# Splitting the last weight load of a decode kernel into eight transfers of fewer partitions

## The chip, the core and the metric

The kernel runs on one core of a Trainium2 chip. The metric is device time in microseconds (us) of one execution; the time given is the median of several runs. The core has TensorE (PE; its weight loads are PEld), VectorE (DVE), ScalarE (ACT), GpSimd (POOL) and SyncE (SP), each with its own instruction stream, and 16 DMA engines that carry the transfers which SyncE and ScalarE issue.

## The reference

One token is decoded. Two branches read the same normalised vector and are added:

```
xn  = layernorm(x)                                  # x: 1 x 1024
q   = xn @ wq                                       # 32 heads of 128
A   = softmax(q k^T / sqrt(128)) v, then @ wo       # 4 KV heads, 65536 cached positions
h   = gelu(layernorm(xn) @ w1)                      # 1024 -> 1024
x1  = xn + shift(h) @ w2                            # four quarters shifted by 1 or 2 places
B   = x1 + gelu(layernorm(x1) @ w3) @ w4            # 1024 -> 3584 -> 1024
out = x + A + B
```

The inputs are bf16. The two caches have 64 MiB each, wq and wo 8 MiB each, w3 and w4 7 MiB each, w1 and w2 2 MiB each. All are read once.

## The kernel before

The host-side code writes out five instruction streams (queues) by hand. A helper records for every buffer object who wrote and who read it, and puts a wait on a semaphore ahead of an instruction only where it is needed and not yet known to be fulfilled. Each load has its own semaphore (a "channel"), and a load is complete when its semaphore has had 16 increments.

The keys and values stream through two slots of 4 MiB each in the tile KV, by 32 loads issued by SyncE. A loop over 32 steps (`NT`) transposes keys on VectorE into the tile WX, multiplies them with the query on TensorE, takes a running maximum and an exponential, and accumulates the values. The weights share these tiles: when the slots come free at the end of the loop, w1 and w2 go into WX, w3 into the first half of KV, wo into the second half, and last w4 into WX again, over w1, w2 and the transposed keys.

A weight of R rows is laid out with R/128 successive rows on each of 128 partitions (`load_rows`, line 328, is one transfer over all 128 partitions). For w4, 3584 x 1024, a partition holds 28 rows of 2 KB. It is loaded in three parts (line 638 on):

```
w4_parts = [(0, 20), (20, 6), (26, 2)]
```

that is 40, 12 and 4 KB a partition, 5120, 1536 and 512 KB in all, each with a buffer object and a semaphore of its own. Their issues wait for the last readers and writers of what they overwrite; behind them SyncE has only the output's store (line 672).

The end of the kernel runs so. After the loop TensorE multiplies with w1 and w2, VectorE does the activation and the second layer norm, TensorE multiplies with w3, and the result `gh_bf` is ready some 24 us before w4 is there. `out_rows` (line 454) then multiplies one row of weights at a time with four matmuls, which add into the PSUM tile `OUT_ps`: first the 32 rows of wo, then, by `w4_pe(i)`, the rows of part 0, 1 and 2 of w4, 80, 24 and 8 matmuls. Each `w4_pe(i)` waits for the semaphore of its part. VectorE casts the sum into `orow` (line 671), SyncE stores it, and the kernel ends.

Of the kernel before, what the change touches and what calls it, by code (L numbers as in the profile page):

```python
# [118 lines left out]
def _deps(q, reads, writes):  # L119
    need = {}  # L120
    for b in reads:
        for s, v in b.w.items():
            need[s] = max(v, need.get(s, 0))
    for b in writes:

        for s, v in (list(b.r.items()) if b.r and b.whole else list(b.w.items()) + list(b.r.items())):
            if not (q.in_order and s is q.sem):
                need[s] = max(v, need.get(s, 0))
    for s, v in need.items():
        q.wait((s, v))  # L130


def _done(ev, reads, writes, partial=False):
    for b in reads:
        b.add_read(ev)
    for b in writes:
        if partial:
            b.add_write(ev)
        else:
            b.set_write(ev)  # L140
# [9 lines left out]
def _grp(q, fns, reads=(), writes=(), partial=False):  # L150
    _deps(q, reads, writes)
    ev = None
    for i, fn in enumerate(fns):
        ev = q.op(fn, i == len(fns) - 1)
    _done(ev, reads, writes, partial)
    return ev
# [8 lines left out]
def _dma(q, chan, fn, reads=(), writes=(), partial=False):  # L165
    _deps(q, reads, writes)
    chan.n += 1
    ev = q.dma(fn, chan.sem, 16 * chan.n)
    _done(ev, reads, writes, partial)
    return ev  # L170


def bass_parallel_sum__gqa_block_cached__mixer_s_mlp__decode_kernel(
# [13 lines left out]
    P = 128  # L187
    D = A_x.shape[2]
# [15 lines left out]
    with ExitStack() as es:  # L204
        E = es.enter_context

        def sb(name, shape, dt):
            return E(nc.sbuf_tensor(name, shape, dt))
# [4 lines left out]
        def sem(name):  # L213
            return E(nc.semaphore(name))
# [47 lines left out]
        gh_bf = sb("gh_bf", [P, KT_F], BF)  # L262
# [4 lines left out]
        WX = sb("WX", [P, 14336 + 16384], BF)  # L267
# [23 lines left out]
        q_sp = _Q("sp", None)  # L291
# [3 lines left out]
        def chan(name):  # L295
            if name not in chans:
                chans[name] = _DmaChan(sem("d_" + name))
            return chans[name]
# [26 lines left out]
        def load_rows(dst, bufs, ch, w, r0, nrow):  # L325
            src = w.rearrange("(p r) n -> p (r n)", p=P)
            ncol = w.shape[1]
            _dma(q_sp, chan(ch), lambda e: e.dma_start(out=dst, in_=src[:, r0 * ncol:(r0 + nrow) * ncol]), writes=bufs)
# [121 lines left out]
        def out_rows(items, reads, last=False):  # L450
            fns = []
            for lhs, rhs in items:
                for jj in range(4):
                    fns.append(lambda e, lhs=lhs, rhs=rhs, jj=jj: e.matmul(  # L454
                        OUT_ps[32 * jj:32 * jj + 1, 0:256], lhs, rhs[:, 256 * jj:256 * jj + 256],
                        start=False, stop=last, tile_position=(0, 32 * jj), skip_group_check=True))
            _grp(q_pe, fns, reads=reads, writes=[b_OUT], partial=True)
# [177 lines left out]
        wo_sb = KV[:, 2:4, :].rearrange("p a c -> p (a c)")  # L635
        load_rows(wo_sb, b_K[1] + b_V[1], "wo", A_wo, 0, 32)
        w4_parts = [(0, 20), (20, 6), (26, 2)]
        b_W4 = [_B() for _ in w4_parts]
        for i, (r0, nr) in enumerate(w4_parts):
            for b in [b_W, b_W2] + b_X[0] + b_X[1]:  # L640
                for d in (b.r, b.w):
                    for s, v in d.items():
                        b_W4[i].add_read((s, v))
            load_rows(WX[:, r0 * D:(r0 + nr) * D], [b_W4[i]], "w4%d" % i, B_w4, r0, nr)

        def w4_pe(i):
            r0, nr = w4_parts[i]
            out_rows([(gh_bf[:, r:r + 1], WX[:, r * D:(r + 1) * D]) for r in range(r0, r0 + nr)], [b_W4[i], b_gh], last=(i == len(w4_parts) - 1))

        _op(q_pe, lambda e: e.matmul(MB_ps[:, 0:HKV], Dmat_f[:, :], keepL[:, :], start=True, stop=True), reads=[b_keep, b_const], writes=[b_MB])  # L650
        _op(q_dve, lambda e: e.reciprocal(cb_rL[:, :], MB_ps[:, 0:HKV]), reads=[b_MB], writes=[b_cb])
# [17 lines left out]
        for i in range(len(w4_parts)):  # L669
            w4_pe(i)  # L670
# [37 lines left out]
```

## Time and profile before

| | before |
|---|---|
| median of 3 runs, us | 403.17 (402.69 to 403.19) |
| profiled execution, us | 402.71 |
| its span, first to last instruction, us | 401.5 |
| mean granted TensorE clock | 0.60 |
| busy: PE / PEld / DVE / ACT / POOL, us | 176.8 / 54.3 / 231.8 / 49.5 / 77.2 |
| read from HBM, MB | 169.87 |
| mean rate over the span, GB/s | 423 |
| DMA packets | 6069 |
| chain that ended last, share of the span | DMA 63%, DVE 21%, PE 11%, ACT 3%, issue 1% |

Times in the profile are us from the start of the span. The chain that ended last is found by going back from the last instruction, at each step to what released it. "Idle before" and the waits name what ended an engine's idle time. The DMA share is the mean busy share of the 16 DMA engines, so one engine working alone shows as 0.06. A row such as "L454 PE MATMUL OUT_ps<-WX,gh_bf" is an operation recorded at line 454 that writes OUT_ps and reads WX and gh_bf. SPq is SyncE's own queue of DMA issues, and "us to landing" is the time from the issue to the last increment of the load's semaphore.

### The profile page before, as it was taken

What the parts mean: (1) busy time and instruction counts of PE and PEld (TensorE: products, weight loads), DVE (VectorE), ACT (ScalarE), POOL (GpSimd) and SP (SyncE); (2) the same over time, 40 slices, a digit from 0 to 9 for tenths busy, and PEclk for the clock granted to TensorE, in tenths of its full rate; (3) what the DMA queues carried; (4) which work ended last, traced back from release to release, by engine and by line L of the source; (5) the groups of instructions that cost most, each with busy time, mean ns of one, the idle gap of its engine ahead of it and who ended that gap; (6) DMA issues with size and microseconds to landing.
All of it is one profiled execution on the core that took longest, in us unless ns stands there. A gap on an engine that the chain in (4) does not pass through costs nothing.

```text
span 401.5 us, 4212 instructions
## 1 busy us (share of the span) xinstructions
PE 176.8 (44%) x1560; PEld 54.3 (14%) x1560; DVE 231.8 (58%) x398; ACT 49.5 (12%) x132; POOL 77.2 (19%) x130
## 2 busy tenths in 40 slices
PE   0432526354444444444435354525363536635055
PEld 0211101011111111111111110101010111321033
DVE  0237566757575857585858585848585857354000
ACT  1000111111111111110202111111111112100000
POOL 5000003121223121112402121114112112320000
PEclk9965555565555565655655656656556556568586
DMA  8999999999999999999999999999999999999993
GB/s 359 424 418 437 444 421 428 455 421 421 444 438 421 432 447 429 418 441 441 424 431 444 431 418 447 438 418 434 447 424 418 454 434 409 463 462 414 422 402 166
DMA packets 6069, 170.02 MB, mean 424 GB/s; under 512 B 804, under 2 KB 808, under 8 KB 936
## 3 DMA queue, kind: packets, MB, share of 16 engines
q1 hardware_dynamic: 5912, 169.87, 98.2%
q8 instruction: 5, 0.08, 0.1%
q14 instruction: 8, 0.07, 0.0%
q10 hardware_dynamic: 144, 0.00, 0.0%
HBM read 169.87 MB, written 0.00 MB: 423 GB/s over the span
## 4 chain that ended last, share of the span: by engine, by line
DMA 63%; DVE 21%; PE 11%; ACT 3%; issue 1%; POOL 0%; ACTq 0%
DMA KV<-in_A_k_cache_dram 49%; DVE WX L495 12%; DMA WX<-in_B_w_dram 11%; PE S_ps L506 4%; DMA x_bf<-in_A_x_dram 3%; DVE pT_f L546 3%; ACT p_sb L536 3%; DVE mrow L513 3%; PE PT_ps L544 2%; PE OUT_ps L454 1%; PE MB_ps L519 1%; PE MM_ps L466 1%; DVE Rm L514 1%; DVE Bst L523 1%; DVE brun L534 1%
## 5 line engine op out<-in xcount | busy, mean ns | idle before, releaser
L495 DVE STREAM_TRANSPOSE WX<-KV 128x1024 f32<-128x1024 f32 x128 | 151.9, 1217 | 63.5 <-DMA KV<-in_A_k_cache_dram 63.5
L553 PE MATMUL OT_ps<-KV,pT_f 128*32 128x512 bf16 x512 | 60.7, 627 | 26.6 <-DVE pT_f L546 25.7
L506 PE MATMUL S_ps<-WX,Ycur 128*32 128x512 bf16 x512 | 58.9, 608 | 17.8 <-DVE WX L495 17.5
L567 POOL TENSOR_TENSOR O_acc<-O_acc,tmpO 128x513 f32<-128x513 f32 x28 | 33.0, 1178 | 89.4 <-ACT tmpO L561 89.4
L565 POOL TENSOR_SCALAR O_acc<-O_acc,ff 128x513 f32<-128x513 f32 x28 | 19.6, 701 | 132.4 <-ACT ff L540 132.4
L519 PE MATMUL MB_ps<-Rm,Lmat 128*128 128x16 bf16 x32 | 6.2, 192 | 83.8 <-DVE Rm L514 83.8
L536 ACT ACTIVATE p_sb<-S_ps,brun 128x512 bf16<-128x512 f32 x32 | 22.0, 688 | 169.3 <-DVE brun L534 142.3
L544 PE MATMUL PT_ps<-p_sb,permR 128*128 128x512 bf16 x32 | 18.2, 568 | 42.4 <-ACT p_sb L536 42.4
L561 ACT ACTIVATE tmpO<-OT_ps 128x512 f32<-128x512 f32 x32 | 19.2, 599 | 105.9 <-PE OT_ps L553 105.9
L513 DVE TENSOR_REDUCE mrow<-S_ps 128x1 f32<-128x512 f32 x32 | 21.5, 673 | 16.6 <-PE S_ps L506 16.6
L546 DVE STREAM_TRANSPOSE pT_f<-PT_ps 128x512 f32<-128x512 f32 x32 | 22.9, 716 | 6.6 <-PE PT_ps L544 6.5
L506 PEld LDWEIGHTS S_ps<-WX,Ycur 128*32 128x32 bf16 x512 | 14.5, 125 | 63.2 <-issue 33.6
L553 PEld LDWEIGHTS OT_ps<-KV,pT_f 128*32 128x32 bf16 x512 | 14.7, 129 | 58.5 <-DVE pT_f L546 29.6
L519 PEld LDWEIGHTS MB_ps<-Rm,Lmat 128*128 128x128 bf16 x32 | 3.3, 102 | 111.0 <-DVE Rm L514 111.0
L671 DVE CAST orow<-OUT_ps 128x256 bf16<-128x256 f32 x1 | 0.4, 425 | 30.0 <-PE OUT_ps L454 30.0
L454 PE MATMUL OUT_ps<-KV,o_bf 128*1 128x256 bf16 x128 | 5.3, 346 | 15.0 <-DMA KV<-in_A_wo_dram 15.0
L523 DVE TENSOR_REDUCE Bst<-MB_ps 128x1 f32<-128x16 f32 x32 | 5.6, 175 | 9.2 <-PE MB_ps L519 9.2
L544 PEld LDWEIGHTS PT_ps<-p_sb,permR 128*128 128x128 bf16 x32 | 3.3, 103 | 45.3 <-ACT p_sb L536 45.3
L384 PE MATMUL MM_ps<-ln_s,ones_f 128*128 128x1 f32 x6 | 1.8, 362 | 17.3 <-DVE ln_s L383 17.3
L454 PE MATMUL OUT_ps<-WX,gh_bf 128*1 128x256 bf16 x112 | 5.7, 395 | 6.7 <-DMA WX<-in_B_w_dram 6.7
L396 POOL TENSOR_TENSOR ln_s<-ln_s,neghalf 128x1 f32<-128x1 f32 x3 | 1.7, 559 | 31.0 <-DVE ln_s L394 31.0
L563 POOL COPY O_acc<-tmpO 128x513 f32<-128x513 f32 x4 | 2.5, 618 | 23.8 <-ACT tmpO L561 23.8
(116 smaller groups left out, 116.3 us busy)
## 6 DMA issues: line engine op xcount, KB each, us to landing
KV<-in_A_k_cache_dram SPq DMA_DIRECT2D x16, 4096.0 KB, 23.4
KV<-in_A_v_cache_dram SPq DMA_DIRECT2D x16, 4096.0 KB, 22.0
KV<-in_A_wq_dram SPq DMA_DIRECT2D x2, 4096.0 KB, 16.7
KV<-in_B_w_dram SPq DMA_DIRECT2D x1, 7168.0 KB, 27.7
WX<-in_B_w_dram SPq DMA_DIRECT2D x1, 5120.0 KB, 42.4
WX<-in_B_w_dram SPq DMA_DIRECT2D x2, 2048.0 KB, 18.4
WX<-in_B_w_dram SPq DMA_DIRECT2D x1, 1536.0 KB, 45.7
WX<-in_B_w_dram SPq DMA_DIRECT2D x1, 512.0 KB, 46.4
```

What stands on the lines that cost most here:

```text
L454: fns.append(lambda e, lhs=lhs, rhs=rhs, jj=jj: e.matmul(OUT_ps[32 * jj:32 * jj + 1, 0:256], lhs, rhs[:, 256 * jj:256 * jj + 256], start=F ...
L495: _op(q_dve, lambda e, ix=ix: e.transpose(out=X32[:, xs, 1024 * ix:1024 * (ix + 1)], in_=KV32[:, 2 * s, 4096 * half + 1024 * ix:4096 * hal ...
L506: fns.append(lambda e, we=we, cm=cm, mv=mv: e.matmul(S_ps[32 * cm:32 * cm + 32, :], Ycur[:, we, :, :].rearrange("p a g -> p (a g)"), mv, s ...
L513: _op(q_dve, lambda e: e.reduce_max(mrow[:, m:m + 1], S_ps[:, :], axis=AX.X), reads=[b_S], writes=[b_mrow[m]])
L519: _op(q_pe, lambda e: e.matmul(MB_ps[:, 0:16], Lmat[:, :], Rm[:, m, :], start=True, stop=True), reads=[b_R[m], b_const], writes=[b_MB])
L536: _op(q_act, lambda e: e.activation(p_sb[:, m, :], S_ps[:, :], ACTF.Exp, bias=brun[:, kn:kn + 1], scale=SCALE, accum_out=tmpO[:, m, 512:513]),
L544: _op(q_pe, lambda e: e.matmul(PT_ps[:, :], permR[:, :], p_sb[:, m, :], start=True, stop=True), reads=[b_p[m], b_const], writes=[b_PT])
L546: _op(q_dve, lambda e: e.transpose(out=pT_f[:, :], in_=PT_ps[:, :]), reads=[b_PT], writes=[b_pT])
L553: fns.append(lambda e, q=q, q4=q4: e.matmul(OT_ps[32 * q4:32 * q4 + 32, :], pT_bf[:, q, :, 1], slot(1, s)[:, 8192 * half + 512 * q:8192 * ...
L561: _op(q_act, lambda e: e.activation(tmpO[:, m, 0:512], OT_ps[:, :], ACTF.Copy), reads=[b_OT], writes=[b_tmpO[m]], partial=True)
L565: _op(q_pool, lambda e: e.tensor_scalar(out=O_acc[:, :], in0=O_acc[:, :], scalar1=ff[:, m:m + 1], scalar2=0.0, op0=ALU.mult, op1=ALU.add), ...
L567: _op(q_pool, lambda e: e.tensor_tensor(out=O_acc[:, :], in0=O_acc[:, :], in1=tmpO[:, m, :], op=ALU.add), reads=[b_tmpO[m]], writes=[b_Oacc])
```

## The change

Parts 0 and 1 of w4 are loaded as before. Part 2, two rows (4 KB) on each of 128 partitions, is loaded by eight transfers instead of one, over successive ranges of 64, 15, 14, 12, 8, 6, 5 and 4 partitions. SyncE issues the eight one after the other, in the place where it issued the one. Each has a buffer object and a semaphore of its own, and the matmuls of part 2 wait for all eight. The sources and destinations, and the matmuls, are the same.

```diff
         w4_parts = [(0, 20), (20, 6), (26, 2)]
-        b_W4 = [_B() for _ in w4_parts]
-        for i, (r0, nr) in enumerate(w4_parts):
+        b_W4 = [_B() for _ in range(10)]
+        for b4 in b_W4:
             for b in [b_W, b_W2] + b_X[0] + b_X[1]:
                 for d in (b.r, b.w):
                     for s, v in d.items():
-                        b_W4[i].add_read((s, v))
-            load_rows(WX[:, r0 * D:(r0 + nr) * D], [b_W4[i]], "w4%d" % i, B_w4, r0, nr)
+                        b4.add_read((s, v))
+        for i, (r0, nr) in enumerate(w4_parts):
+            if i < 2:
+                load_rows(WX[:, r0 * D:(r0 + nr) * D], [b_W4[i]], "w4%d" % i, B_w4, r0, nr)
+                continue
+            p0 = 0
+            for j, n in enumerate((64, 15, 14, 12, 8, 6, 5, 4)):
+                src = B_w4.rearrange("(p r) n -> p (r n)", p=P)[p0:p0 + n, r0 * D:(r0 + nr) * D]
+                _dma(q_sp, chan("w4%d%d" % (i, j)), lambda e, p0=p0, n=n, src=src: e.dma_start(out=WX[p0:p0 + n, r0 * D:(r0 + nr) * D], in_=src),
+                     writes=[b_W4[i + j]])
+                p0 += n
+            assert p0 == P
 
         def w4_pe(i):
             r0, nr = w4_parts[i]
-            out_rows([...], [b_W4[i], b_gh], last=(i == len(w4_parts) - 1))
+            out_rows([...], (b_W4[i:i + 1] if i < 2 else b_W4[2:]) + [b_gh], last=(i == len(w4_parts) - 1))
```

More of the change, by code (lines that the diff above doesn't have):

```diff
@@ L642, in bass_parallel_sum__gqa_block_cached__mixer_s_mlp__decode_kernel @@
                     for s, v in d.items():
-                        b_W4[i].add_read((s, v))
-            load_rows(WX[:, r0 * D:(r0 + nr) * D], [b_W4[i]], "w4%d" % i, B_w4, r0, nr)
+                        b4.add_read((s, v))
[10 more added lines that the diff above has]
+            assert p0 == P
         def w4_pe(i):
             r0, nr = w4_parts[i]
-            out_rows([(gh_bf[:, r:r + 1], WX[:, r * D:(r + 1) * D]) for r in range(r0, r0 + nr)], [b_W4[i], b_gh], last=(i == len(w4_parts) - 1))
+            out_rows([(gh_bf[:, r:r + 1], WX[:, r * D:(r + 1) * D]) for r in range(r0, r0 + nr)], (b_W4[i:i + 1] if i < 2 else b_W4[2:]) + [b_gh], last=(i == len(w4_parts) - 1))
         _op(q_pe, lambda e: e.matmul(MB_ps[:, 0:HKV], Dmat_f[:, :], keepL[:, :], start=True, stop=True), reads=[b_keep, b_const], writes=[b_MB])
```

## Prediction

> **What bounds the kernel now.** I read the page first, then the chain of waits for the last 12 us, the waits, the table by windows, and last the DMA issues. On the page the DMA row is at 9 tenths in 38 of 40 slices, so the time is set by loading 170 MB, and only what follows the last bytes can be moved by an edit to the last transfer. The end of the chain, as pieces in order of time (start us, us, what):
>
> ```profile
> 351.14 42.43 DMA WX<-in_B_w_dram
> 393.57 0.04 issue
> 393.62 5.71 PE OUT_ps L454 x109
> 399.33 0.02 issue
> 399.35 0.42 DVE orow L671
> ```
>
> The chain waits for a load of WX that was issued at 351.14, then follows TensorE without a break for 5.71 us, then VectorE and the output. Which load it is stands in the DMA issues of that stretch (size, us to landing):
>
> ```profile
> WX<-in_B_w_dram SPq DMA_DIRECT2D x1, 5120.0 KB, 42.4
> WX<-in_B_w_dram SPq DMA_DIRECT2D x1, 1536.0 KB, 45.7
> WX<-in_B_w_dram SPq DMA_DIRECT2D x1, 512.0 KB, 46.4
> ```
>
> The first is part 0 of w4 (20 rows a partition), landing at 393.57. Part 1 (6 rows), issued at 351.52, lands at 397.2; part 2 (2 rows, 4 KB a partition), issued at 352.00, at 398.42. The change touches part 2 alone, and the chain doesn't pass through it. The waits after 388 us say the same:
>
> ```profile
> DVE orow L671 <- PE OUT_ps L454: 30.0, 1, 30.0
> PEld OUT_ps L454 <- DMA WX<-in_B_w_dram: 7.0, 1, 7.0
> PE OUT_ps L454 <- DMA WX<-in_B_w_dram: 6.7, 1, 6.7
> ```
>
> One wait of TensorE for WX, not three: parts 1 and 2 were there when it came to them. In the records the first matmul of part 2 has its wait at 398.80, 0.38 us after the landing. This slack is the number on which everything hangs. The windows show why it is small and who lands last (us; PE busy, PEld busy, DVE, ACT, POOL; clock, DMA share, GB/s):
>
> ```profile
> 395.00:395.50 0.50, 0.50 (x19) 0.28 (x10) 0.00 (x0) 0.00 (x0) 0.00 (x0) 0.50 0.44 180
> 396.00:396.50 0.50, 0.50 (x16) 0.33 (x12) 0.00 (x0) 0.00 (x0) 0.00 (x0) 0.50 0.16 66
> 397.00:397.50 0.50, 0.50 (x16) 0.34 (x12) 0.00 (x0) 0.00 (x0) 0.00 (x0) 0.50 0.06 25
> 397.50:398.00 0.50, 0.50 (x16) 0.32 (x12) 0.00 (x0) 0.00 (x0) 0.00 (x0) 0.50 0.06 25
> ```
>
> TensorE is busy throughout at half clock. A share of 0.06 is one of 16 DMA engines: after 396.6 a single late engine carries the tail. The completion records of part 2 say so exactly: nine of its 16 increments come at 395.02 to 395.44, six at 396.15 to 396.63, the last at 398.42. That engine needs 0.155 us for each 4 KB row, alone as well as beside the 15 others, so its 26 GB/s isn't a limit that all share.
>
> **The change, part by part.** Instead of 128 rows as 8 on each engine, the 64-partition transfer gives every engine 4, and the other 64 rows go out as 15, 14, 12, 8, 6, 5 and 4. How many engines a short transfer uses can be counted on the page: queue q1 has 5912 packets, 41 loads of 128 rows and 16 completions make 5904, and the output's four partitions leave 8, four rows and four completions. So n partitions under 16 are taken to use n engines, one row each. An engine then moves 4 rows at least and 4 + 7 = 11 at most, where it had 8. The late one gains up to 4 x 0.155 = 0.62 us or loses up to 3 x 0.155 = 0.47 us. The Trainium skill ("DMA: Bandwidth & Descriptors", section on why a DMA increments its semaphore by 16) says that the lowest-numbered k engines are used, which would make engine 15 the one with 4 rows; no record here numbers the late engine.
>
> *SyncE.* Seven more issues. The rows nearest are 0.43 us for a WX load and 0.62 for the four-partition output: 3.0 to 4.3 us, from 352.4 to at most 356.8. Queued behind them is only the output's issue at 399.80, and the engines have earlier bytes until 393.4. Cost: nothing, 43 us of cover. The waits ahead of the eight are the same semaphores as before.
>
> *TensorE.* Part 2's matmuls wait on eight semaphores instead of one. One goes with the weight load; seven more are instructions of their own, 51 ns each in the records (386.03 is one). They stand behind part 1's matmuls and ahead of the eight of part 2. If all eight have landed early, TensorE's backlog hides them; those that stand after the last to land cost up to 7 x 0.051 = 0.36 us. I take three, 0.15 us, near the middle of 0 and 0.36.
>
> *More, shorter transfers.* Where one load of an engine follows another in the trace (12 KB rows, then 4 KB rows), the next row starts within 0.02 us of the completion packet. Seven boundaries more: 0.14 us at most. Upper end: if each single row had to complete, at the 0.37 us from the late engine's last byte (398.05) to its landing (398.42), before the next began, 7 x 0.37 = 2.6 us. I take nothing, since 41 loads follow one another without this gap.
>
> *Who writes where.* In every load of the trace each engine carries eight rows of all 128 partitions, so the 0.155 us may be the engine's limit or that of the eight partitions it writes; no row separates them. This is the unknown that decides.
> If it is the engine's, the late engine's part 2 lands between 398.42 - 0.62 = 397.80 and 398.42 + 0.47 = 398.89. TensorE comes at 398.80: cost 0 to 0.3 us with the waits. It can't be a gain at this clock, since TensorE's run starts from part 0, which isn't touched.
> If it is the partitions', moving rows to another engine relieves nothing. The eight partitions behind the late engine still have to take part 1 (8 rows at 0.46) and part 2 (8 at 0.155), whoever brings them: the early engines' rows come in from 393.4 and hold up the late engine's part 1 by up to 8 x 0.155 = 1.24 us. Besides, the late engine now has 4 to 11 rows for other partitions: 0.62 to 1.7 us after 398.42, so 399.04 to 400.13. I take 7 rows (the 64 and three of the seven short ones): 398.42 + 1.09 = 399.50. Add 0.04 from landing to matmul (the chain's issue row) and 0.15 for the waits: part 2 starts at 399.69 instead of 398.80, 0.89 us late. Part 1, landing at up to 397.21 + 1.24 = 398.45, is wanted at 397.63, and TensorE idles there too, but within the same delay: 24 matmuls at half clock (1.17 us) bring it to about 399.6.
>
> I take the second case, because the lone engine between 397 and 398 runs no faster than in the crowd: the limit lies on its own way to the memory. The Trainium skill speaks against the change at this point: "SBUF — State Buffer", section on Door 1, says that partitions 0 to 63 reach only 8 of 16 DMA ports, and gives 196 GB/s for them against 328 for all 128 at 1 MiB. By that page each port takes 27.2 GB/s, a row of 4 KB 0.151 us, and the sum is the second case's; no run here shows a load of fewer partitions at full load.
>
> **The sum.** The profiled execution took 402.71, 1.2 us more than its span of 401.5, and is at the low end of the runs shown (402.69, 403.17, 403.19). Its sum is 402.71 + 0.89 = 403.60; on the median, 403.17 + 0.89 = 404.06, forecast 404.1.
>
> **Rivals.** *Covered* (chance 0.22): the limit is the engine's, or sharing costs less than the slack allows. Part 2 lands at 397.8 to 398.9 and TensorE's 5.4 us of matmuls from 393.62 set the end: 403.2, up to 403.5. For it: no wait for part 2 in the profile. Against: the slack is only 0.38 us. It decides as long as part 2 lands before 398.8.
> *Faster through a faster clock* (0.08, the other side): the clock is granted in turns, 0.50 until 398.67 and 1.0 after it. Where an execution has the full clock at 393.6, four matmuls take 0.109 instead of 0.213 us, TensorE is through part 1 by 397.9, and part 2's landing at 398.42 ends the chain; then 4 rows less on the late engine bring 0.5 us: 402.7. To exceed 0.2% it needs a later late engine than in this profile, one more of the 1 us lags by which it fell behind: 402.2.
> *Serial single rows* (0.10): the 0.37 us above, paid by a late engine that is in all seven: 396.81 + 0.62 + 7 x 0.53 + 0.37 = 401.5, 2.7 us late, 405.9.
> *Not spread at all* (0.02): 64 rows on one engine would take 9.9 us, landing at 404.3, 408.7 in all; the packet count above speaks against it.
>
> **How the numbers follow.** The forecast, partitions limited, has 0.58; its own range on the median is 403.4 (landing at 399.04, the waits hidden) to 404.9 (400.13 and 0.36 us of waits). 0.2%, 0.8 us, is about what a measurement of this kernel can tell from no change; the point 403.97 lies a little above the first third of that range, so 0.41 of the 0.58 is slower and 0.17 the same. Slower: 0.41, and 0.12 of the two last rivals, 0.53. Same: 0.17, the 0.22 of Covered, and 0.03 of the clock rival, whose gain mostly stays under 0.8 us: 0.42. Faster: 0.05. The range runs from 402.7 (Covered at the level of the lowest run) to 405.1, which leaves out the two last rivals and the faster end.
>
> **What would show it.** In the changed profile SyncE issues ten loads of w4, the last by 357 us; that is certain. If the forecast is right, the waits show a second wait of TensorE for WX after 397 us, of 0.5 to 1 us; the DMA share between 395 and 397 is above the 0.44 and 0.16 of before while fewer GB/s move than engines are busy; rows of 4 KB take longer than 0.155 us. If Covered is right, the chain is the five pieces above with the same 5.7 us, and rows take 0.155 us. I am wrong if part 2 lands before 398.8 and the time still grows, or if the load of part 0 lands at another time than 393.6: then something ahead of the change moved.

## The result and the profile after

The changed kernel takes 405.00 us (median of 5 runs, 404.86 to 405.22) against 402.77 us before (402.69 to 403.19): a ratio of 1.0053 with a 95% interval of 1.0038 to 1.0068, slower by 2.2 us. Its profiled execution has a span of 403.94 us, 2.5 us more than the 401.47 before.

The end of the chain of waits (start us, us, what):

```profile
354.59 46.42 DMA WX<-in_B_w_dram
401.01 0.14 issue
401.14 0.62 PE OUT_ps L454 x6
401.77 0.02 issue
401.79 0.42 DVE orow L681
```

Before, the chain went through part 0's landing and 5.7 us of TensorE. Now it goes through the last of the eight transfers, issued at 354.59 and landed at 401.01, and TensorE has only part 2 left behind it. TensorE's groups in order of time (start, us, ... count, idle time before and what ended it) show where it lost its lead:

```profile
393.62 4.16 PE L454 MATMUL OUT_ps<-WX,gh_bf 128*1 128x256 bf16 x80 [5.70 <-DMA WX<-in_B_w_dram]
399.27 0.82 PE L454 MATMUL OUT_ps<-WX,gh_bf 128*1 128x256 bf16 x24 [1.48 <-DMA WX<-in_B_w_dram]
401.14 0.60 PE L454 MATMUL OUT_ps<-WX,gh_bf 128*1 128x256 bf16 x8 [1.05 <-DMA WX<-in_B_w_dram]
```

Part 0 starts at 393.62 as before. Part 1, a plain transfer that the diff doesn't touch, lands at 399.22 instead of 397.21 and keeps TensorE idle for 1.48 us. Part 2 lands at 401.01 instead of 398.42 and costs another 1.05 us. The DMA engines in half-microsecond windows (length, TensorE busy, its clock, DMA share, GB/s):

```profile
394.00:394.50 0.50, 0.50 (x18) 0.50 1.69 279
394.50:395.00 0.50, 0.50 (x16) 0.50 0.70 90
395.00:395.50 0.50, 0.50 (x18) 0.50 0.73 115
```

and the same of the kernel before:

```profile
394.00:394.50 0.50, 0.50 (x16) 0.50 1.06 442
394.50:395.00 0.50, 0.50 (x16) 0.50 0.86 352
395.00:395.50 0.50, 0.50 (x19) 0.50 0.44 180
```

A packet is counted whole in the window where it starts, so a share can exceed 1 and one window alone overstates the loss. Over the microsecond from 394 to 395 the engines move about 185 GB/s at a mean share of 1.20, against 397 at 0.96 before: as busy, with less than half the bytes. In the packet records every 12 KB row of part 1 took 0.46 us before; now 19 of the 128 take longer, up to 1.39 us. The 4 KB rows of part 2 took 0.159 us each (0.155 from start to start), and now up to 0.55 us.

The page's queue line confirms how the short transfers are spread:

```profile
q1 hardware_dynamic: 5976, 169.87, 97.9%
```

40 plain loads make 5760 packets, the 64-partition one 80, the seven short ones 64 rows, and the output 8; 64 remain, a completion for each of the 64 rows. So n partitions under 16 do run on n engines.

### The profile page after: what moved, and what is told of

Read it like the earlier page. It is cut to its first block, busy times and chain, and to the rows that moved or that the text cites. A ratio compares the mean times of both kernels' runs of the same rounds, so it can differ in the third digit from the quotient of the medians.

```text
span 403.9 us, 4223 instructions
## 1 busy us (share of the span) xinstructions
PE 178.2 (44%) x1560; PEld 54.5 (13%) x1560; DVE 231.8 (57%) x398; ACT 49.4 (12%) x132; POOL 76.9 (19%) x130
## 4 chain that ended last, share of the span: by engine, by line
DMA 64%; DVE 21%; PE 9%; ACT 3%; issue 1%; SPq 1%; ACTq 0%
DMA KV<-in_A_k_cache_dram 50%; DVE WX L495 12%; DMA WX<-in_B_w_dram 11%; PE S_ps L506 4%; DVE pT_f L546 3%; DMA KV<-in_A_wq_dram 3%; DVE mrow L513 3%; ACT p_sb L536 3%; PE PT_ps L544 2%; PE MB_ps L519 1%; DVE Bst L523 1%; DVE Rm L514 1%; DVE brun L534 1%; SPq L651 1%; PE MM_ps L466 1%
## 5 line engine op out<-in xcount | busy, mean ns | idle before, releaser
L454 PE MATMUL OUT_ps<-KV,o_bf 128*1 128x256 bf16 x128 | 6.4, 392 | 13.8 <-DMA KV<-in_A_wo_dram 13.8
L421 PE MATMUL PT_ps<-KV,xn_bf 128*32 128x512 bf16 x32 | 4.9, 609 | 8.1 <-DMA KV<-in_A_wq_dram 8.1
```

The costliest lines, as they stand in the source:

```text
L454: fns.append(lambda e, lhs=lhs, rhs=rhs, jj=jj: e.matmul(OUT_ps[32 * jj:32 * jj + 1, 0:256], lhs, rhs[:, 256 * jj:256 * jj + 256], start=F ...
```

## The experiments

Three theories of the 2.2 us. **Crossing**: an engine that writes rows outside the partitions which it has in a plain 128-partition transfer collides with others, slowing both (the first expectations call it Sharing). **Number**: each further transfer costs, whatever its shape. **Late engine**: only the extra rows on the engine that is last anyway count. In all kernels but the five-part one, part 2 is a list of pieces, each a range of partitions and a range of columns with its own semaphore:

```
for j, (ps_, cs_) in enumerate(pieces):
    _dma(q_sp, ..., e.dma_start(out=WX[ps_, cs_], in_=w4_src[ps_, cs_]), writes=[b_W4[i + j]])
```

`ALL` stands below for the 2048 columns of rows 26 and 27, and the diffs are shortened to the pieces and what else changes. Landings of before are 393.57, 397.21 and 398.42 for parts 0, 1 and 2.

### Eight transfers, all of 128 partitions

```diff
-(64, 15, 14, 12, 8, 6, 5, 4) partitions x ALL
+[(slice(0, P), slice(r0 * D + 256 * j, r0 * D + 256 * j + 256)) for j in range(8)]
```

> Part 2 as eight transfers like the change, but each over all 128 partitions and 256 of the 2048 columns: eight issues, eight semaphores, eight waits, no short range of partitions, 8 x 512 B on each engine each time. Sharing theory (several engines writing into the same few partitions slow each other and hold up part 1): nothing is shared, part 1 lands at 397.2 as before, part 2 at 398.4 to 399.0, the time is that of before to +0.4 us. Number theory (each further transfer costs, whatever its shape): about the +2.2 us of the change. Late-engine theory (only the three extra rows on the late engine count): no change, its bytes are those of before.

402.86 us, ratio 1.0013 (1.0004 to 1.0021), 0.5 us. Part 1 lands at 397.22, no 12 KB row takes over 0.465 us, and part 2 lands at 398.70:

```profile
397.26 0.53 PEld L454 LDWEIGHTS OUT_ps<-WX,gh_bf 128*1 128x1 bf16 x24 [0.17 <-DMA WX<-in_B_w_dram]
398.84 0.39 PE L454 MATMUL OUT_ps<-WX,gh_bf 128*1 128x256 bf16 x8 [0.75 <-DMA WX<-in_B_w_dram]
```

```profile
394.50:395.00 0.50, 0.50 (x16) 0.50 0.91 287
395.00:395.50 0.50, 0.50 (x20) 0.50 0.63 192
```

Eight transfers, eight semaphores and eight waits cost about a quarter of the loss (two fifths at the upper end of the interval), and they don't hold up part 1: as the main cause, the Number theory falls. What the number does cost is seen at the last landing, 0.28 us later than before.

### Eight ranges of 16 successive partitions

```diff
+[(slice(16 * j, 16 * j + 16), ALL) for j in range(8)]
```

> Part 2 as eight transfers of 16 successive partitions each, so every engine has 8 rows of 4 KB as before, but four engines at a time go to neighbouring partitions. Sharing theory: nearly as bad as the change, part 1 lands near 399, part 2 near 400.5, time +1.5 to +2 us. Number theory: +2.2 us. Late-engine theory: no change, since no engine has an extra row.

404.57 us, ratio 1.0049 (1.0036 to 1.0062), 2.0 us. Part 1 lands at 399.15, part 2 at 400.62:

```profile
399.19 0.83 PE L454 MATMUL OUT_ps<-WX,gh_bf 128*1 128x256 bf16 x24 [0.91 <-DMA WX<-in_B_w_dram]
400.76 0.39 PE L454 MATMUL OUT_ps<-WX,gh_bf 128*1 128x256 bf16 x8 [0.74 <-DMA WX<-in_B_w_dram]
```

The two waits of the change are there although no engine has an extra row. The Late-engine theory can't be more than a small part: about the 0.39 us by which part 2 lands sooner here than with the change.

### The same with every eighth partition

```diff
+[(slice(j, P, 8), ALL) for j in range(8)]
```

> As the eight transfers of 16 partitions, but each takes every eighth partition (j, j+8, ...), so the sixteen rows of a transfer are spread over the whole range. The same issues, rows, bytes and waits as with successive partitions. Sharing theory: about half the sharing, rows of 4 KB near 0.31 us where they meet, part 2 at about 399.5, time +0.5 to +1 us. Number theory: +2.2 us, as with successive ones. Late-engine theory: no change.

405.46 us, ratio 1.0068 (1.0055 to 1.0081), 2.7 us; part 1 at 399.92, part 2 at 401.41. Spreading the sixteen rows over the whole range helped nothing. So it isn't how near to each other the rows of one transfer lie; that half of my expectation was wrong.

### Two halves

```diff
+[(slice(64 * j, 64 * j + 64), ALL) for j in range(2)]
```

> Part 2 as two transfers of 64 partitions, 0 to 63 and 64 to 127: 4 + 4 rows on every engine. Sharing theory: in each half two engines meet in the same partitions, rows near 0.31 us, part 2 at 398.8 to 399.6, time +0.2 to +0.8 us. Number theory: one transfer more, +0.3 us. Late-engine theory: no change.

404.73 us, ratio 1.0062 (1.0046 to 1.0077), 2.5 us. One cut through the partitions, with 4 + 4 rows on every engine, does all the harm that the eight did: part 1 at 399.46, part 2 at 400.56. In the windows:

```profile
394.50:395.00 0.50, 0.50 (x20) 0.50 0.94 131
395.00:395.50 0.50, 0.50 (x16) 0.50 0.67 131
```

The expected 0.2 to 0.8 us had assumed that two engines that meet share fairly.

### The halves from another source

```diff
-in_=w4_src[ps_, cs_]
+in_=w1_src[ps_, 0:nr * D]      # 4 KB rows, one after the other
```

> The two halves of 64 partitions again, but their rows are read from one contiguous stretch of w1 (4 KB after 4 KB) instead of from w4 (4 KB every 56 KB), so the last two rows of w4 are replaced by other numbers; destinations, sizes and waits are those of the halves. If the slowing comes from where the rows are written (sharing at the destination): as with the halves, part 1's last landing near 399.5, part 2 near 400.6. If it comes from the order in which memory is read: it changes, most likely towards 397.2 and 398.4.

404.7 us in one run, where the kernel before has 403.0. Part 1 lands at 399.64, part 2 at 400.75, 12 KB rows up to 1.36 us: the numbers of the halves. Reading 4 KB after 4 KB instead of every 56 KB changes nothing, so the collision isn't one of those addresses in memory. What the halves have in common is where they write, and that an engine has four rows of a transfer instead of eight; no record says which partitions an engine writes, so that engines meet in the same ones is inferred, not seen.

Another record points to the writing. Behind its last row of a load an engine has a completion packet, and from its start to the increment of the semaphore the mean over all loads of w4 is 0.35 us before, 0.37 with the column pieces and 0.35 with the five plain parts below. It is 0.71 with the change, 0.76 with ranges of 16, 0.83 with every eighth partition, 0.66 and 0.65 with the two kernels of halves, 0.54 with half the dose below. The rows are not only slower to send: they land later after they were sent.

### Half the dose

```diff
+[(slice(0, P), row 26)] + [(slice(64 * j, 64 * j + 64), row 27) for j in range(2)]
```

> Row 26 of part 2 as one plain transfer over 128 partitions, only row 27 (2 KB a partition) as two halves of 64. Crossing theory (rows that an engine writes outside the partitions which it has in a plain transfer collide): half the bytes cross, part 1 is held up by half, about 1 us, part 2 near 399.5, time +0.8 to +1.3 us. If any short transfer costs a fixed amount: the full +2.2 us of the halves. Late-engine theory: no change.

403.36 us, ratio 1.0016 (1.0007 to 1.0025), 0.65 us; part 1 at 398.10, part 2 at 399.21. The hold-up of part 1 is 0.89 us, where it is 2.25 with all of part 2 in halves: it goes with the bytes that cross, somewhat faster than in proportion, and a fixed price for a short transfer doesn't fit.

### The halves in the middle of the stream

```diff
-for i in part 0, part 1, part 2
+for i in part 2 (two halves), part 0, part 1
```

> The two halves, issued ahead of parts 0 and 1 instead of behind them, so that they run in the middle of the stream. The order alone makes part 0 land 1.24 us later than before (394.8) and part 1 last, at 398.4. Crossing theory: the 128 rows take about twice their time on every engine, and the stream behind them is late by that, 1.2 to 2.5 us: part 0 at 396 to 397.3, part 1 at 399.6 to 401. If the harm needs the uneven tail (early engines colliding with a late one): 394.8 and 398.4 hold.

407.9 us in one run. Part 0 lands at 398.61 and part 1, now the last, at 402.23: 3.8 us later than the 398.42 of the same bytes before. The windows around the halves, and those of the kernel before:

```profile
377.00:379.00 2.00, 0.00 (x0) 0.50 0.46 115
379.00:381.00 2.00, 0.00 (x0) 0.50 1.38 317
```

```profile
377.00:379.00 2.00, 0.00 (x0) 0.50 0.65 279
379.00:381.00 2.00, 0.00 (x0) 0.50 1.18 512
```

The stream loses and never catches up, and the load of wo that runs beside the halves lands 3 us later as well (384.45, not 381.50). The harm doesn't need the tail of the stream, and the price is above my 1.2 to 2.5 us. That the engines are uneven may still matter in it: before, wo's completions come from 378.02 to 381.50, so the last engine lags there too.

### By themselves, on idle engines

```diff
+q_sp.wait(part 1 landed)
 for j, (ps_, cs_) in enumerate(pieces):
```

with the pieces plain, as halves, and as the change's eight.

> Part 2 as one transfer over 128 partitions, but issued only when part 1 has landed, so that it runs on idle engines: the control for the next two. All theories: rows of 4 KB take 0.155 to 0.16 us each, the 16 engines start and end together, 1.24 us from the first row's start to the last row's end; the whole kernel ends some 2 to 3 us later than before, from the wait.

> The two halves of 64 partitions issued only when part 1 has landed: no other transfer is in flight but the two. If two engines share each group of partitions by the shape of the transfer alone: rows of 0.31 us, 2.5 us from first start to last end. If the harm needs a plain transfer still running beside it: rows of 0.16 us, 1.24 us as in the control. If a transfer more costs a fixed amount: rows of 0.16 us and a gap between the halves.

> The eight transfers of the change (64, 15, 14, 12, 8, 6, 5, 4 partitions) issued only when part 1 has landed. By the shape of the transfers alone: 0.31 us a row in the 64, up to 0.62 us in the short ones, where up to four engines write to neighbouring partitions, unless the 0.3 to 0.6 us between their issues on SyncE keeps them apart; 3 to 5.6 us in all. If the harm needs a plain transfer beside it: rows of 0.16 us throughout.

From SyncE's issue, 15 of the 16 engines have landed the plain transfer after 3.4 us (397.50 to 400.88); the sixteenth comes at 402.19, of which more below. The halves are there after 4.8 us (397.40 to 402.17) and the eight after 6.0 (397.33 to 403.29). The control isn't as even as expected: its first rows take up to 0.98 us, and its 15 engines need 2.1 us for their rows, not 1.24.

Against the 15 engines the halves need 1.4 us more. Of these, 0.4 pass before the first row, which starts 1.35 us after the issue instead of 0.96; the other 1.0 lies between the first row and the last landing. Once the start is over, most rows of the first half take 0.159 us and most of the second 0.22 to 0.30, and from the completion packet to the increment both halves need 0.84 us, against 0.31 in the control. So two halves are slowed with no other load beside them, in one run, and by no more than the 1.24 us of sharing by two. For the eight, SyncE's 4.3 us of issuing is in the 6.0, and after 399.5 rows take up to 0.38 us: the 0.62 of four at one place wasn't seen. The three runs took 406.2, 406.4 and 407.5 us, against 402.4 for the kernel before; the wait alone cost 3.8 us, not 2 to 3.

### Five plain parts

```diff
-w4_parts = [(0, 20), (20, 6), (26, 2)]
+w4_parts = [(0, 12), (12, 8), (20, 4), (24, 3), (27, 1)]
```

> w4 in five plain transfers of 12, 8, 4, 3 and 1 rows over all 128 partitions instead of 20, 6 and 2: the last engine's bytes and order are those of before, but TensorE starts 5 us sooner and has only four matmuls left behind the last landing. All theories: two more transfers of the plain form cost at most 0.1 us at the landing; the end comes 0.1 us (clock full) to 0.4 us (clock half) sooner than before, ratio 0.999 to 1.000. Number theory: +0.5 us.

402.53 us, ratio 0.9991 (0.9982 to 1.0000), 0.4 us, at the edge of what can be measured. Part 4 lands at 398.49, 0.07 us later than part 2 before, and TensorE is done 0.35 us sooner (the cast begins at 399.00 instead of 399.35):

```profile
397.92 1.02 PE L454 MATMUL OUT_ps<-WX,gh_bf 128*1 128x256 bf16 x16 [0.79 <-DMA WX<-in_B_w_dram]
399.00 0.42 DVE L671 CAST orow<-OUT_ps 128x256 bf16<-128x256 f32 x1 [29.86 <-PE OUT_ps L454]
```

Cutting by columns is nearly free, and if this end can be shortened by a cut, it is by this one.

## Why the prediction was right, and what it mis-sized

The direction and the case chosen (*who writes where*: moving rows to another engine relieves nothing and holds up part 1) held as far as these runs can tell, and 405.00 lies inside 402.7 to 405.1. That it does is luck: forecast and range stand on a median of 403.17 before, and this time the kernel before took 402.77. As differences, 0.89 us was forecast and 1.9 was the top of the range, against 2.2 measured, and 405.00 lies above the 404.9 that the chosen case had as its own upper end. The ground given for the choice was luck too. That the lone engine runs no faster than in the crowd holds in either case, and it doesn't tell an engine's limit from that of the partitions it writes.

*The signs.* They came, larger than named: a wait of 1.48 us for part 1 and one of 1.05 for part 2, where one of 0.5 to 1 was expected, a DMA share of 0.73 at 395.00 where it was 0.44, and rows of 4 KB up to 0.55 us.

*Part 0, SyncE.* As predicted part 0's run begins at 393.62, and SyncE is through its issues at 354.89, 3.4 us for eight.

*TensorE's waits.* 0.15 us taken. Four semaphore instructions stand in the records, not seven (two waits go into one), and behind the last landing only one of them: 0.14 us from landing to matmul, 0.04 before. The term is 0.10.

*More, shorter transfers.* Taken as nothing. In the records its seven boundaries cost 0.006 us each. The increments of the late engine come 0.18 to 0.19 us apart, though, for rows that start 0.161 apart, so that the way from its last byte to its landing grows to 0.60 us, from 0.37 before. The eight column pieces show this price by itself: 0.28 us later.

*Own rows of the late engine.* Seven taken out of 4 to 11, eleven measured: each of the eight transfers has a last completion between 399.72 and 401.01, well behind its others, so the late engine is one of the four that even the 4-partition transfer uses. In the records its eleven rows follow one another from 398.66 to 400.41, 1.75 us where 1.09 was taken. Against before, three rows more are 0.47 us.

*The hold-up of part 1.* At most 1.24 us was allowed, on the ground that eight partitions pass their rows at the same rate, whoever brings them. The late engine reaches its first row of part 2 at 398.66, not 396.81: 1.85 us. With halves part 1 is held up by 2.25 us although every engine has 4 + 4 rows, and in mid-stream the cost is 3.8: beside other loads more is lost than by a fair share.

So two terms were mis-sized about equally. Told from the late engine's first row of part 2 in the kernel before, the predicted landing is 396.81 + 1.24 + 1.09 + 0.37 = 399.51, the measured one 396.81 + 1.85 + 1.75 + 0.60 = 401.01: 0.61 us from the hold-up, 0.66 from the rows, 0.23 from the last byte to the landing. Part 2 thus lands 2.59 us later than before. The slack takes 0.38 of it and the way from landing to matmul adds 0.14, so its matmuls begin 2.34 us later (401.14, not 398.80). In the profile shown they also meet a clock that is back at half from 400.8, take 0.6 us instead of 0.5, and the cast begins 2.44 us later.

*The rivals.* Covered fails: the slack of 0.38 us is gone many times over. (It counted 5.4 us of TensorE's matmuls, which is the weight loads' time; the matmuls take 5.7.) Serial single rows, at 405.9, was as near to the measured 405.0 as the forecast of 404.1, so the time alone doesn't decide against it. The records do: its 0.37 us a row are not between the late engine's completions, and it leaves part 1 where it was. Not spread fails by the packet count. The faster clock was seen, in the run with eight column pieces: there the clock was full from 396.58, TensorE waited for a last landing at 398.70, and the chain went through part 2's landing. That the end before is TensorE's alone is thus a matter of the clock's turn in the one profile shown.

*Against the page.* The Trainium skill, "SBUF — State Buffer", Door 1, had the sign: partitions 0 to 63 alone are slower than all 128. Its sizes don't fit beside other transfers: 8 ports at its 27.2 GB/s would be an estimated 218 GB/s, the halves and the plain rows beside them moved 131 in the windows above. By its table 16 successive partitions reach 4 ports and every eighth reaches 8, and yet the second was not faster (1.0068 against 1.0049). Why meeting engines lose more than their share, and by what map they meet, stays open.

## What to carry to other kernels

Cut a transfer by columns, with all 128 partitions in every piece; a cut through the partitions slowed itself and the plain transfers that ran beside it (most likely because engines then meet in the same partitions), and cost the stream more than its own bytes. In a kernel that is bound by its loads, look for the DMA engine that lands last (a share of 0.06 in the windows) before balancing the tail by hand, and for the slack that the consumer has there: here, at the clock of the profile before, TensorE's own run would have hidden what a better balance could bring. Where transfers collide beside others, a sum that assumes fair sharing was too low here.

## What was not expected of the hardware

The late engine seems to be made by code loading. In the kernel before, the 16 completions of a load spread over 0.40 us at 32 us and over 1.9 us at 41.5, with instruction packets of 16 and 8 KB at 36.7 and 38.9 between them; the spread goes from 1.7 to 2.6 us around the packet at 260.8 and from 2.5 to 3.5 around that at 358.8, and in between it shrinks by 0.2 us at most. Other such packets, at 340.3, 363.8 and 368.1 among them, leave it as it was; perhaps they ran on other engines, but no record numbers the engine. On idle engines it can be seen alone: a 16 KB instruction packet starts at 398.68 and takes 1.37 us beside the plain transfer, and one of the 16 engines lands 1.3 us behind the rest.

SyncE can be held up by its own issues: the eight column pieces, each of 128 rows of 512 B, were issued over 39.6 us, the eight of other shapes over 3.4 to 5.0.

```profile
350.98 39.57 SPq L651 DMA_DIRECT2D WX<-in_B_w_dram  x8
```

The last three issues end at 363.96, 379.96 and 390.55, each close to an earlier load's landing (done at 362.17; 377.91 to 381.47; 389.99 to 393.55), as if they waited for room behind loads under way; no run tests this. It did no harm, since the last issue was done at 390.55, before the pieces were due; nothing else stood behind them on SyncE.
